# Attention with a fused feed-forward on one core: a column maximum taken by DVE block transposes and spread by a diagonal matmul

## The chip, the cores and the metric

One of the eight cores of a Trainium2 chip runs the whole program. The metric is the device time of one execution in microseconds. Five engines work side by side, each through its own list of instructions in order: PE (TensorE: matmuls and transposes), DVE (VectorE), ACT (ScalarE), POOL (GpSimd) and SP, which issues the DMAs. PSUM is the memory that PE writes; SBUF holds the rest.

## The reference

Attention over 8 batches and 8 heads, with the queries pooled in pairs, and behind it a feed-forward layer with a maximum of three products:

```python
q_pool = q.reshape(B, H, S // 2, 2, D).mean(axis=3)          # B 8, H 8, S 1152, D 64
scores = scale * np.matmul(q_pool, k.transpose(0, 1, 3, 2))  # 576 x 1152 for each head
scores = scores - np.max(scores, axis=-1, keepdims=True)
attn = np.exp(scores)
attn = attn / (np.sum(attn, axis=-1, keepdims=True) + 1e-09)
attn_out = np.matmul(attn, v)
x = attn_out.transpose(0, 2, 1, 3).reshape(B * S_pooled, H * D)   # 4608 tokens x 512
h = np.maximum(np.maximum(x @ w1, x @ w2), x @ w3)                # 512 -> 768
out = h @ w_out                                                   # 768 -> 512
```

All of it in float32.

## The kernel before, in words

**Tiling.** The attention is cut into 64 units, numbered d = 0 to 63: a batch (8), a pair of heads (4), and a half of 288 of the 576 pooled queries (2). In a unit the scores lie transposed: the 128 partitions are keys, the columns are 2 heads x 288 queries = 576. Nine blocks of 128 keys (`kk`) make up the 1152 keys. The feed-forward runs in chunks of 512 tokens, each once the batch that holds its tokens is done; the chunks are fitted between the units of the next batch, and the last of them follow behind the last unit.

**A unit.** For each `kk`, PE multiplies keys and queries into the PSUM tile `pqk`. Queries and keys are split into a high and a low part in float32r (lines 542 and 543: four matmuls of 288 columns for each `kk`). ACT copies `pqk` to the SBUF tile `s` (line 548), and DVE folds it into the running maximum `acc` (lines 554 and 557), one tile of 128 x 576 that exists once (`bufs=1`).

After the ninth block, `acc` holds a maximum over every 128th key, and what is wanted is the maximum over its partitions, for each of the 576 columns, and that in all partitions, because it has to be subtracted from `s`. This is done in two halves `h` of 345 and 231 columns, that is 3 and 2 blocks of 115:

- `rows` (line 593): PE transposes each block of `acc` into the PSUM tile `pmt`, so that a column becomes a partition;
- `reduce` (line 599, step `red`): DVE takes the maximum along the free axis into `m`, one number for each query;
- `bcast` (line 609, step `bc`): PE transposes `m`, repeated 128 times, into the PSUM tile `pmb`, so that each partition holds all the maxima of the half.

Both PSUM tiles of half 0 take the one buffer of `ps_a`, those of half 1 the one buffer of `ps_b`. Half 1 also waits until ACT has copied the attention output of the unit before out of `ps_b` (`xout[d - 1]`).

Then DVE subtracts (`sub`, line 624), ACT takes the exponential (`exp`, line 630), six pieces each. POOL adds the nine blocks of `s` into `ksum` (`key`, lines 643 and 645); PE multiplies `s` by the values into `pav` (`product` in `values`, line 673: 18 products, 36 matmuls), and sums `ksum` over the partitions with a matmul of ones (`total`, line 687). DVE takes the reciprocal (line 694), POOL scales (line 697), ACT and POOL split the result into `xh` and `xl` (lines 772 and 775) for the feed-forward. Up to unit 15 (`EARLY`) the sums are taken in another way, with small matmuls. `s` has six buffers of three blocks, enough for two units.

The feed-forward multiplies with split weights: `ph` (line 935) for the three inner products, `po` (line 990) for the outer one. With chunk 0, which runs beside units 8 and on, the weights are converted from 64-bit floats, mostly on DVE.

**Order.** The instructions are not issued in the order of the loops. Each piece of work is a `Step` with the engine that can do it, a cost in us, and the steps it has to follow. `arrange` is a list scheduler: it plays the steps through with these costs and picks, whenever an engine is free, the ready step with the lowest rank. The rank is the unit's number plus an offset for the kind of step (`RANK`) plus one for the single step (`NUDGE`). The order that comes out is fixed for each engine; on the chip an engine waits where an operand is late. The DMAs of the queries, keys, values and weights are issued by SP in that order too; POOL issues none.

Of the kernel before, what the change touches and what calls it, by code (L numbers as in the profile page):

```python
# [18 lines left out]
P = 128  # L19
# [3 lines left out]
QH = 288  # L23
CB = 115
DM = 512
# [11 lines left out]
    "qk": -364.0396,  # L37
    "cp": -126.5549,
    "mx": -318.2574,
    "rows": -969.9796,  # L40
    "red": -172.0313,
    "bc": -345.8464,
    "sub": 215.1752,
    "exp": 196.9402,
    "keys": -671.9276,
    "av": 14.8431,
    "xcopy": -516.1778,
    "psum": 398.4083,
    "eps": 343.2889,
    "inv": 357.0576,  # L50
    "xm": -706.0274,
    "load": 386.6538,
    "prep": 638.9001,
    "move": 1290.4425,
    "split": 283.1141,
    "ffn": -33.8173,
    "rate": 1.047,
    "mm": 49.0387,
    "fetch": 603.0832,
    "evac": -724.5554,  # L60
    "hhigh": 1228.3483,
    "hlow": -714.7034,
    "conv": 648.8915,
    "rate0": 4.5084,
    "first_qk": -97.1625,
    "first_cp": -630.79,
    "first_mx": 212.4188,
    "first_sub": 204.5779,
    "first_exp": 244.1512,
    "first_keys": -1118.9276,  # L70
    "first_av": 141.406,
    "first_xcopy": -152.0387,
    "first_psum": 65.359,
    "first_inv": 141.5566,
    "first_xm": 829.3378,
    "first_load": -197.5173,
    "first_prep": 180.1798,
    "first_move": -1436.3679,
    "first_split": 375.0794,
# [209 lines left out]
def pe(n):  # L289
    return ("pe", n * 1e-3)  # L290
# [784 lines left out]
```

## Time and profile before

| | |
|---|---|
| median of 3 runs | 1474.91 us (1472.44 to 1477.5) |
| profiled execution, its own time | 1472.96 us |
| span of the profiled execution, first to last instruction | 1471.1 us |
| mean granted clock of PE | 0.978 |
| PE busy | 1398.0 us (95%) |
| weight loads (PEld) | 1098.5 us (75%) |
| DVE busy | 1044.0 us (71%) |
| ACT busy | 902.5 us (61%) |
| POOL busy | 1079.1 us (73%) |

How to read the rows that follow. PE, PEld, DVE, ACT, POOL and SP are the engines; PEld is the loading of weights, which overlaps the matmuls. `L593` is line 593 of the kernel. A group row reads: line, engine, operation, output <- inputs, shape of the output <- shape of the first input, count | busy us, mean ns of one | us in which the engine was idle just before, and for whom it waited. A timeline row reads: start in us, length in us, engine, line, operation, tiles, count, and in brackets the idle time before. A wait row reads: who waited <- for whom: us in all, times, longest. The granted clock is the share of its full clock that PE was allowed. In a row by stretches the stretch and its length come first, then for PE, PEld, DVE, ACT and POOL the busy time with the number of instructions. Matmul ends are modelled and overlap, so a busy PE is not PE at its peak.

### The profile page before, as it was taken

Reading aid. Unit: us, or ns where it says so; the run is one execution under the profiler, and the core shown is the slowest. Engines: PE = TensorE matmul, PEld = TensorE weight load, DVE = VectorE, ACT = ScalarE, POOL = GpSimd, SP = SyncE. Lnnn points to the kernel's source line nnn. Section 1 sums busy time; section 2 is a strip of 40 time slices with the busy share of each in tenths; the row PEclk is TensorE's granted clock in tenths of the full one; section 3 lists DMA queues with packets and bytes.
Section 4 is the critical chain, followed back from the end, with each engine's and each line's share of the span. In section 5 each row is a group of like instructions: output and inputs, shape, how many; then the busy total and the mean of one; then the engine's idle time right before and its main releaser. Section 6 shows DMA issues by size and latency. Waiting matters only on the chain.

```text
span 1471.1 us, 24704 instructions
## 1 busy us (share of the span) xinstructions
PE 1398.0 (95%) x8704; PEld 1098.5 (75%) x8704; DVE 1044.0 (71%) x1441; ACT 902.5 (61%) x1464; POOL 1079.1 (73%) x835
## 2 busy tenths in 40 slices
PE   4888999898899999999999999999999999999999
PEld 4566677675677878777777777777777777878999
DVE  3897789898877767777688778777787768861110
ACT  3776776567666666567566766666766757651211
POOL 1897975889868878679888878888787978772210
PEclk9988999998899999999999999999999999999999
DMA  6675456576456656565567556664566556414441
GB/s 181 169 203 147 122 153 207 184 206 194 118 151 185 201 155 182 168 181 148 148 192 203 152 145 191 182 182 134 163 189 184 149 148 185 144 69 162 149 161 59
DMA packets 114762, 240.71 MB, mean 164 GB/s; under 512 B 15440, under 2 KB 75216, under 8 KB 114640
## 3 DMA queue, kind: packets, MB, share of 16 engines
q1 hardware_dynamic: 114064, 238.55, 55.8%
q8 instruction: 70, 1.15, 0.3%
q10 hardware_dynamic: 576, 0.59, 0.2%
q14 instruction: 52, 0.43, 0.1%
HBM read 144.70 MB, written 18.87 MB: 111 GB/s over the span
## 4 chain that ended last, share of the span: by engine, by line
PE 75%; DVE 10%; DMA 4%; ACT 4%; issue 4%; POOL 2%; SPq 1%; ACTq 0%; DVEq 0%; POOLq 0%
PE ph L935 28%; PE pav L673 14%; PE po L990 10%; PE pqk L542 9%; PE pqk L543 8%; DVE s L624 3%; DVE acc L557 3%; DMA kraw<-in_kT_dram 2%; PE pmt L593 2%; PE psum L687 2%; PE pmb L609 2%; POOL ksum L645 1%; ACT s L548 1%; DVE w L848 1%; DVE w L843 1%
## 5 line engine op out<-in xcount | busy, mean ns | idle before, releaser
L645 POOL TENSOR_TENSOR ksum<-ksum,s 128x576 f32<-128x576 f32 x448 | 638.2, 1425 | 26.1 <-ACT s L630 3.5
L935 PE MATMUL ph<-xh,w 128*128 128x512 f32 (+2 forms) x1440 | 464.3, 376 | 2.7 <-DVE w L868 1.3
L548 ACT COPY s<-pqk 128x576 f32<-128x576 f32 x576 | 362.4, 639 | 103.4 <-PE pqk L543 97.8
L624 DVE TENSOR_TENSOR s<-s,pmb 128x693 f32<-128x693 f32 (+1 forms) x384 | 395.1, 1049 | 39.5 <-PE pmb L609 38.3
L542 PE MATMUL pqk<-qq,kc 128*128 128x288 f32 x1152 | 357.9, 326 | 56.1 <-DVE acc L557 30.7
L557 DVE TENSOR_TENSOR acc<-acc,pqk 128x576 f32<-128x576 f32 x448 | 335.3, 749 | 82.8 <-ACT s L548 78.1
L630 ACT ACTIVATE s<-s 128x693 f32<-128x693 f32 (+1 forms) x384 | 352.5, 933 | 41.9 <-DVE s L624 38.6
L543 PE MATMUL pqk<-qq,kc 128*128 128x288 f32 x1152 | 332.3, 303 | 0.0
L542 PEld LDWEIGHTS pqk<-qq,kc 128*128 128x128 f32 x1152 | 225.6, 196 | 113.7 <-DVE acc L557 44.5
L673 PE MATMUL pav<-s,v 128*64 128x288 f32 x2304 | 306.8, 418 | 1.3 <-ACT s L630 1.0
L935 PEld LDWEIGHTS ph<-xh,w 128*128 128x128 f32 x1440 | 263.1, 188 | 41.4 <-ACT xr L682 1.8
L935 PE MATMUL ph<-xl,w 128*128 128x512 f32 (+2 forms) x720 | 268.3, 373 | 0.0
L673 PEld LDWEIGHTS pav<-s,v 128*64 128x64 f32 x2304 | 165.2, 140 | 119.3 <-issue 16.6
L543 PEld LDWEIGHTS pqk<-qq,kc 128*128 128x128 f32 x1152 | 227.5, 197 | 10.4
L643 POOL TENSOR_TENSOR ksum<-s 128x576 f32<-128x576 f32 x64 | 92.0, 1437 | 107.8 <-ACT s L630 104.8
L956 DVE TENSOR_TENSOR hm<-hm,ph 128x512 f32<-128x512 f32 (+2 forms) x120 | 75.8, 631 | 126.8 <-PE ph L935 124.8
L966 POOL TENSOR_TENSOR h_lo<-hm,h_hi 128x512 fp32r<-128x512 f32 (+2 forms) x60 | 70.6, 1176 | 126.1 <-ACT h_hi L963 123.6
L935 PEld LDWEIGHTS ph<-xl,w 128*128 128x128 f32 x720 | 135.8, 189 | 11.5
L438 POOL TENSOR_TENSOR kraw<-kraw 128x1152 fp32r<-128x1152 f32 x31 | 82.8, 2670 | 63.1 <-DMA qraw<-in_qT_dram 26.6
L599 DVE TENSOR_REDUCE m<-pmt 116x3 f32<-116x384 f32 (+1 forms) x128 | 61.3, 488 | 89.9 <-PE pmt L593 89.8
L682 ACT COPY xr<-pav 128x288 f32<-128x288 f32 x64 | 25.5, 399 | 147.0 <-PE pav L673 146.9
L694 DVE RECIPROCAL rs<-rs 128x288 f32<-128x288 f32 (+1 forms) x64 | 96.5, 1507 | 17.7 <-ACT rs L691 17.3
(57 smaller groups left out, 1293.6 us busy)
## 6 DMA issues: line engine op xcount, KB each, us to landing
w<-w_split SPq DMA_DIRECT2D x144, 512.0 KB, 3.6
kc<-kraw SPq DMA_DIRECT2D x384, 96.0 KB, 2.2
qq<-qraw SPq DMA_DIRECT2D x252, 144.0 KB, 3.3
v<-in_vr_dram SPq DMA_DIRECT2D x32, 576.0 KB, 3.8
kraw<-in_kT_dram SPq DMA_DIRECT2D x31, 576.0 KB, 6.0
qraw<-in_qT_dram SPq DMA_DIRECT2D x31, 576.0 KB, 4.0
w<-in_win_dram SPq DMA_DIRECT2D x18, 512.0 KB, 5.9
w_split<-w SPq DMA_DIRECT2D x18, 512.0 KB, 5.5
```

The lines of the kernel that those rows point to most:

```text
L542: nc.tensor.matmul(ps[:, h - hs[0], :QH], w, qq[:, 0, h], start=True, stop=False)
L543: nc.tensor.matmul(ps[:, h - hs[0], :QH], w, qq[:, 1, h], start=False, stop=True)
L548: nc.scalar.copy(o.s[kk // 3][:, kk % 3, slice(*hs)], o.ps[kk, hs][:, :, :QH])
L557: nc.vector.tensor_tensor(acc, acc, ps, op=ALU.max)
L624: nc.vector.tensor_tensor(s, s, o.pb[h][:, None, :w].broadcast_to([P, 3, w]), op=ALU.subtract)
L630: nc.scalar.activation(s, s, AF.Exp, scale=SCALE)
L643: vec[e].tensor_tensor(o.ksum, o.s[0][:, 0], x, op=ALU.add)
L645: vec[e].tensor_tensor(o.ksum, o.ksum, x, op=ALU.add)
L673: nc.tensor.matmul(o.pav[64 * h : 64 * h + 64, :QH], pr.v[:, kk, h], o.s[kk // 3][:, kk % 3, h], start=(kk == 0), stop=(kk == NK - 1),)
L694: nc.vector.reciprocal(o.rs, o.rs)
L935: nc.tensor.matmul(t.ps[:, : hi - lo], w[:, a, kk], xx[:, kk, lo:hi], start=(kk == 0 and i == 0), stop=(kk == 3 and i == 2),)
L990: nc.tensor.matmul(t.ps[:, : hi - lo], ww[:, kk, ms], hh[:, kk, lo:hi], start=(kk == 0 and i == 0), stop=(kk == 5 and i == 2),)
```

## The change

From unit 16 (`TURN`) on, `rows`, `reduce` and `bcast` are replaced:

- `fold`: one DVE reduction over `acc`, seen as 18 blocks of 32 columns, with `apply_transpose`. It transposes 32 x 32 blocks, so that the maximum is taken over each group of 32 partitions. The result, in `crest`, is 128 partitions x 18: partition 32 g + q, column t holds the maximum over partition group g for column 32 t + q.
- `turn`: one PE transpose of `crest`, 128 x 128, into `ps_a`.
- `summit`: one DVE reduction over the four groups, 18 x 32 maxima in PSUM.
- `m_high` on ACT and `m_low` on DVE split them into a high and a low float32r part, in partitions 0 to 17 and 32 to 49 of `parts2`.
- `spread_out`: one POOL multiplication of `pick` (a diagonal, both parts below each other) with `parts2` makes `diag`, 64 x (18 x 32), which is zero except where the row is the block's own.
- `bcast_wide`: two matmuls of a matrix of ones (`wide`, 128 x 128) with halves of `diag`, 288 columns each, put the sum of both parts into all 128 partitions. The halves are now 288 and 288 columns.

The next unit's first maximum into `acc` now waits for `fold` instead of both `rows`. `blank`, a DVE step at about unit 12, sets `pick` and zeroes the new tiles. Units 0 to 15 keep the old way. All numbers in `RANK` and `NUDGE` are others, so the order of every step can differ; the scheduler and its cost model are the same. The host code gives the program a smaller scratch for DMA descriptors.

```diff
+SQ = 32
+NB = 18
+TURN = 16
...
+    wide = cpool.tile([P, P], F32R, name="wide")
+    nc.vector.memset(wide.bitcast(F32), 1.0)
+    pick = cpool.tile([2 * SQ, NB], F32, name="pick")
+    crest = [cpool.tile([P, P], F32, name=f"crest{i}") for i in range(2)]
+    parts2 = [cpool.tile([2 * SQ, SQ], F32R, name=f"parts{i}") for i in range(2)]
+    diag = [cpool.tile([P, NB, SQ], F32R, name=f"diag{i}") for i in range(2)]
+
+    def blank():
+        for i in range(2):
+            rows = slice(SQ * i, SQ * i + SQ)
+            nc.vector.tensor_copy(pick[rows], ident[rows, SQ * i : SQ * i + NB])
+            nc.vector.memset(crest[i], 0.0)
+            nc.vector.memset(parts2[i].bitcast(F32), 0.0)
+            nc.vector.memset(diag[i].bitcast(F32), 0.0)
...
+    blanks = step("top", TURN - 4, [("dve", 3.2)], lambda e: blank(), [])
...
-                    after = [c] + ([copies[0]] + (old.rows if old else []) if kk == 1 else [tops[-1]])
+                    after = [c] + ([copies[0]] + (old.accread if old else []) if kk == 1 else [tops[-1]])
...
-        for h, (x0, x1) in enumerate([(0, 3 * CB), (3 * CB, 2 * QH)]):
+        late = d >= TURN
+        spans = [(0, QH), (QH, 2 * QH)] if late else [(0, 3 * CB), (3 * CB, 2 * QH)]
+        free_a = old.subs[0] if old else []
...
+        def fold(e):
+            nc.vector.tensor_reduce(
+                crest[d % 2][:, :NB],
+                o.acc.rearrange("p h q -> p (h q)").rearrange("p (t k) -> p t k", t=NB),
+                axis=AX.X, op=ALU.max, apply_transpose=True,
+            )
+
+        def turn(e):
+            o.pb[0] = ps_a.tile([P, 512], F32, tag="a", name=f"pmb{d}_0")
+            nc.tensor.transpose(o.pb[0][:, QH : QH + P], crest[d % 2], ident)
+
+        def summit(e):
+            o.top = o.pb[0][:NB, QH + P : QH + P + SQ]
+            nc.vector.tensor_reduce(
+                o.top, o.pb[0][:NB, QH : QH + P].rearrange("p (g k) -> p k g", g=4), axis=AX.X, op=ALU.max
+            )
+
+        def m_high(e):
+            nc.scalar.copy(parts2[d % 2][:NB], o.top)
+
+        def m_low(e):
+            nc.vector.tensor_tensor(parts2[d % 2][SQ : SQ + NB], o.top, parts2[d % 2][:NB], op=ALU.subtract)
+
+        def spread_out(e):
+            nc.gpsimd.tensor_tensor(
+                diag[d % 2][: 2 * SQ],
+                pick[:, :, None].broadcast_to([2 * SQ, NB, SQ]),
+                parts2[d % 2][:, None, :].broadcast_to([2 * SQ, NB, SQ]),
+                op=ALU.mult,
+            )
+
+        if late:
+            x = step("red", d, [("dve", 0.775)], fold, [tops[-1], blanks, getattr(old2, "turned", None)])
+            o.accread = [x]
+            x = o.turned = step("turn", d, [pe(150)], turn, [x] + free_a)
+            x = step("top", d, [("dve", 0.25)], summit, [x])
+            y = step("top", d, [("act", 0.2)], m_high, [x] + getattr(old2, "full", []))
+            x = step("top", d, [("dve", 0.17)], m_low, [x, y] + getattr(old2, "full", []))
+            full = step("diag", d, [("pool", 1.16)], spread_out, [x, y] + getattr(old2, "bcs", []))
...
+            def bcast_wide(e, h=h):
+                if h:
+                    o.pb[h] = ps_b.tile([P, 512], F32, tag="b", name=f"pmb{d}_{h}")
+                half = diag[d % 2][:, NB // 2 * h : NB // 2 * h + NB // 2]
+                nc.tensor.matmul(o.pb[h][:, :QH], wide, half.rearrange("p t k -> p (t k)"), start=True, stop=True)
...
+            if late:
+                b = step("bc", d + 0.1 * h, [pe(145)], bcast_wide, [full, gone] + (old.subs[1] if h else []), cols=QH)
```

More of the change, by code (lines that the diff above doesn't have):

```diff
@@ L36 @@
 RANK = {
[L37 to L79, printed above, removed]
+    "qk": -486.7374,
+    "cp": -103.3155,
+    "mx": -288.9473,
+    "rows": -790.567,
+    "turn": -659.5712,
+    "top": -182.8625,
+    "diag": -294.5856,
+    "red": -185.4375,
+    "bc": -601.717,
+    "sub": -61.1511,
+    "exp": 460.2444,
+    "keys": -280.409,
+    "av": -26.5486,
+    "xcopy": -292.3542,
+    "psum": 615.1834,
+    "eps": 886.2793,
+    "inv": 80.4537,
+    "xm": -555.9621,
+    "load": 502.0497,
+    "prep": 791.2287,
+    "move": 1196.0834,
+    "split": 125.478,
+    "ffn": 89.1205,
+    "rate": 5.3966,
+    "mm": 187.8282,
+    "fetch": 1021.9249,
+    "evac": -862.1647,
+    "hhigh": 563.7857,
+    "hlow": -491.662,
+    "conv": 581.7571,
+    "rate0": 6.3552,
+    "first_qk": 117.0643,
+    "first_cp": -304.3318,
+    "first_mx": -78.9748,
+    "first_sub": 607.3251,
+    "first_exp": -247.6462,
+    "first_keys": -231.2583,
+    "first_av": 681.3599,
+    "first_xcopy": -315.4183,
+    "first_psum": 75.5781,
+    "first_inv": 571.8784,
+    "first_xm": 774.8629,
+    "first_load": -542.1866,
+    "first_prep": -282.0663,
+    "first_move": -1397.9498,
+    "first_split": 676.8054,
 }
 NUDGE = {
[81 rows of a table removed]
[85 rows of a table added]
 }
@@ L585, in scores @@
         pools = (ps_a, ps_b)
-        for h, (x0, x1) in enumerate([(0, 3 * CB), (3 * CB, 2 * QH)]):
+        late = d >= TURN
+        spans = [(0, QH), (QH, 2 * QH)] if late else [(0, 3 * CB), (3 * CB, 2 * QH)]
+        free_a = old.subs[0] if old else []
+        bc = {}
+        def fold(e):
+            nc.vector.tensor_reduce(
+                crest[d % 2][:, :NB],
+                o.acc.rearrange("p h q -> p (h q)").rearrange("p (t k) -> p t k", t=NB),
+                axis=AX.X,
+                op=ALU.max,
+                apply_transpose=True,
+            )
[26 more added lines that the diff above has]
+            full = step("diag", d, [("pool", 1.16)], spread_out, [x, y] + getattr(old2, "bcs", []))
+            o.full = [full]
+            o.bcs = []
+        for h, (x0, x1) in enumerate(spans):
             nb, w = 3 - h, x1 - x0
@@ L613, in bcast @@
                     )
-            gone = xout[d - 1] if d > SPLIT and h else None
-            x = step("rows", d + 0.1 * h, [pe(133 * nb)], rows, [tops[-1], gone] + (old.subs[h] if old else []))
-            o.rows.append(x)
-            x = step("red", d, [("dve", 0.067 + nb * 0.133)], reduce, [x])
-            b = step("bc", d + 0.1 * h, [pe(89 + 99 * nb)], bcast, [x])
+            def bcast_wide(e, h=h):
+                if h:
+                    o.pb[h] = ps_b.tile([P, 512], F32, tag="b", name=f"pmb{d}_{h}")
+                half = diag[d % 2][:, NB // 2 * h : NB // 2 * h + NB // 2]
+                nc.tensor.matmul(
+                    o.pb[h][:, :QH], wide, half.rearrange("p t k -> p (t k)"), start=True, stop=True
+                )
+            gone = xout[d - 1] if d > SPLIT and h else None
+            if late:
+                b = step("bc", d + 0.1 * h, [pe(145)], bcast_wide, [full, gone] + (old.subs[1] if h else []), cols=QH)
+                o.bcs.append(b)
+            else:
+                x = step(
+                    "rows", d + 0.1 * h, [pe(133 * nb)], rows, [tops[-1], gone] + (old.subs[h] if old else [])
+                )
+                o.rows.append(x)
+                x = step("red", d, [("dve", 0.067 + nb * 0.133)], reduce, [x])
+                b = step("bc", d + 0.1 * h, [pe(89 + 99 * nb)], bcast, [x])
             for i in range(3):
@@ L635, in scores @@
                 o.exps[i, h] = step("exp", r, [("act", 0.109 + w / 400)], exp, [x])
+        if not late:
+            o.accread = o.rows
         o.sums = []
@@ L1059 @@
     from concourse.bass_utils import run_bass_kernel_spmd
-    nc = bacc.Bacc("TRN2", target_bir_lowering=False, num_devices=1)
+    nc = bacc.Bacc("TRN2", target_bir_lowering=False, num_devices=1, dynamic_dma_scratch_size=1024)
     arrays, args = {}, []
```

166 rows, old and new, of the table NUDGE are left out of this document.

## The prediction

> **What bounds the kernel now.** I read the page first, then the busy time by stretches of the span, then TensorE's own timeline, because the change takes TensorE work away and adds work to the other engines.
>
> ```profile
> span 1471.1 us, 24704 instructions
> PE 1398.0 (95%) x8704; PEld 1098.5 (75%) x8704; DVE 1044.0 (71%) x1441; ACT 902.5 (61%) x1464; POOL 1079.1 (73%) x835
> ```
>
> Busy time by stretch (columns: PE, PEld, DVE, ACT, POOL, granted clock, DMA share, GB/s):
>
> ```profile
> 0.00:300.00 300.00, 251.44 (x1636) 187.40 (x1636) 242.49 (x405) 198.50 (x316) 220.52 (x163) 0.94 0.59 168
> 200.00:300.00 100.00, 91.28 (x588) 70.13 (x586) 93.15 (x171) 65.06 (x111) 72.66 (x53) 0.98 0.61 187
> 300.00:400.00 100.00, 86.22 (x530) 63.98 (x530) 92.05 (x163) 70.99 (x123) 86.78 (x71) 0.86 0.64 185
> 400.00:1311.00 911.00, 903.55 (x5561) 700.81 (x5560) 681.12 (x831) 599.66 (x958) 730.64 (x560) 1.00 0.58 166
> ```
>
> From 400 us on TensorE is busy 903.55 of 911 us at full clock; DVE has 230 us free there, ACT 311, POOL 180. TensorE is the bound in that stretch, so what it sheds there should shorten the span. Before 400 us it isn't: between 200 and 400 us DVE is busy 92 to 93% and TensorE waits, with a clock that drops to 0.86. The transposes that the change removes, counted by stretch (PE columns first), say where the changed units lie:
>
> ```profile
> 0.00:300.00 300.00, 11.41 (x70) 8.11 (x70) 12.82 (x28) 0.94 0.59 168
> 300.00:400.00 100.00, 5.21 (x25) 3.16 (x25) 4.66 (x10) 0.86 0.64 185
> 400.00:1311.00 911.00, 40.38 (x225) 26.27 (x225) 43.58 (x90) 1.00 0.58 166
> ```
>
> Five `pmt` transposes belong to a unit: 14 units lie before 300 us, 5 between 300 and 400, 45 behind. Units 16, 17 and 18 are thus changed in the stretch that DVE holds, and 45 of the 48 changed units where TensorE is the bound.
>
> **The change part by part.** *Removed from TensorE.* A duration is not what an instruction occupies, since matmuls overlap; the starts tell. Two places, one of each kind:
>
> ```profile
> 845.73 0.39 PE L990 MATMUL po<-h_lo,wo_hi 128*128 128x512 f32 x1
> 845.96 0.39 PE L990 MATMUL po<-h_hi,wo_lo 128*128 128x512 f32 x1
> 846.19 0.49 PE L593 MATMUL pmt<-ident,acc 128*116 128x128 f32 x3
> 846.43 0.38 PE L542 MATMUL pqk<-qq,kc 128*128 128x288 f32 x1
> 846.65 0.29 PE L543 MATMUL pqk<-qq,kc 128*128 128x288 f32 x1
> 846.78 0.29 PE L542 MATMUL pqk<-qq,kc 128*128 128x288 f32 x1
> ...
> 872.12 0.29 PE L543 MATMUL pqk<-qq,kc 128*128 128x288 f32 x1
> 872.25 0.66 PE L609 MATMUL pmb<-ident,m 116*128 116x116 f32 x5
> 872.68 0.48 PE L935 MATMUL ph<-xh,w 128*128 128x512 f32 x1
> 873.00 0.40 PE L935 MATMUL ph<-xl,w 128*128 128x512 f32 x1
> ```
>
> A `po` matmul occupies 0.23 us (845.73 to 845.96) and a `pqk` 0.13 (846.65 to 846.78). From 845.96 to the second `pqk` are 0.69 us; less 0.23 and 0.13, three transposes cost 0.33, or 0.11 each. The first `pqk` behind them is included, as it starts early and takes longer. From 872.12 to the second `ph` are 0.88 us; less 0.13 and 0.23 (a `ph` has the 512 columns of a `po`), five `pmb` cost 0.52, or 0.104 each. A unit sheds 5 x 0.11 + 5 x 0.104 = 1.07 us.
>
> *Added to TensorE.* One transpose `turn` of 128 columns: from 0.11 (as now) to 0.12 (0.11 x 128/116); I take 0.12. Two matmuls of 288 float32r columns with 128x128 weights: that is the shape of `pqk`, 0.13 each. The upper end is that they run in two passes as `pav` does, 36 matmuls for 18 products:
>
> ```profile
> 705.95 4.59 PE L673 MATMUL pav<-s,v 128*64 128x288 f32 x36
> ```
>
> That is 0.255 a product. I take 0.13, since weights and moving operand are float32r as in `pqk`. Net per unit: 1.07 - 0.12 - 0.26 = 0.69 us; 45 units make 31.0 us; with the two-pass price it would be 0.44, or 20 us. For the three units between 300 and 400 us I count half of 2.1, 1 us.
>
> *DVE, ACT, POOL.* Rows of units 40 to 47, by shape, and single rows of the whole span:
>
> ```profile
> L593 PE MATMUL pmt<-ident,acc 128*116 128x128 f32 x42 | 7.7, 280 | 0.7 <-ACT xr L682 0.7
> L609 PE MATMUL pmb<-ident,m 116*128 116x116 f32 x40 | 6.6, 266 | 0.0
> L557 DVE TENSOR_TENSOR acc<-acc,pqk 128x576 f32<-128x576 f32 x56 | 41.9, 749 | 7.9 <-ACT s L548 7.2
> L599 DVE TENSOR_REDUCE m<-pmt 116x3 f32<-116x384 f32 x8 | 4.5, 557 | 14.2 <-PE pmt L593 14.2
> L599 DVE TENSOR_REDUCE m<-pmt 116x2 f32<-116x256 f32 x8 | 3.4, 423 | 1.9 <-PE pmt L593 1.9
> L772 ACT CAST xh<-xr 128x32 fp32r<-128x32 f32 x4 | 0.9, 218 | 0.0
> L645 POOL TENSOR_TENSOR ksum<-ksum,s 128x576 f32<-128x576 f32 x56 | 79.8, 1425 | 2.7
> ...
> L714 DVE TENSOR_SCALAR rs<-psum 96x6 f32<-96x6 f32 x16 | 2.4, 152 | 1.8 <-PE psum L704 1.7
> L338 DVE MEMSET ones<- 128x64 f32 x1 | 0.1, 112 | 0.8 <-PEq L1061 0.8
> L340 DVE MEMSET eps<- 128x1 f32 x1 | 0.1, 59 | 0.0
> ```
>
> DVE sheds two reductions, 0.557 + 0.423 = 0.98 us. It gains the fold over 576 elements: the two reductions grow by 0.134 per 128 elements, so 576 make 0.76; no row has the block-transposing form, and twice that, 1.5, is my upper end, for a pass of its own for the transpose. `top` reads 128 elements from PSUM: 0.29 by the same line. `m_low` is a small subtraction: 0.15 to 0.2. Together 1.25, so 0.27 more, 12 us in the 45 units, against 230 free: hidden by TensorE. With the upper end it is 45 us, still hidden. ACT gains `m_high`, 0.22 us, 10 us against 311. POOL gains `spread_out`, 576 elements from two inputs: the 1.43 us of `ksum`; the diff's planner puts 1.16, the lower end. That is 64 us, so POOL would be busy 795 of some 880 us, 90% instead of 80%. The cover is POOL's 180 free us; without it, each unit pays 1.43.
>
> The second half's `bc` keeps its waits for the copied `pav` of the unit before and for that unit's subtractions. The `sub` and `exp` pieces become 864 wide instead of 1035 and 693, the same elements: nothing.
>
> `blank` puts memsets and copies on DVE near unit 12, where DVE is the bound: from 0.112 and 0.059 a memset costs 0.06 + 0.84 ns an element, so 128, 576 and 32 wide with a small copy, twice, 1.8 us; I count 2 in full. `wide` is set at the start behind the first loads. The scratch size changes no instruction, and no DMA is added or moved past another.
>
> *The longer chain and the waits.* Now a unit's maximum goes DVE, PE, DVE, PE, DVE, in two halves that overlap. Then it goes DVE (0.76), PE (0.12), DVE (0.29), ACT (0.22), DVE (0.2), POOL (1.43), PE (0.13): 3.2 us without the handovers, and POOL works in order, so `spread_out` also waits for the `ksum` additions queued before it, up to 1.43 us for each. Behind a waiting `bc` on TensorE stand the next `pqk` or `ph`, and all six `sub` wait for it. What covers it is seen in unit 43:
>
> ```profile
> 886.16 0.75 DVE L557 TENSOR_TENSOR acc<-acc,pqk 128x576 f32<-128x576 f32 x1
> 887.31 0.54 PE L593 MATMUL pmt<-ident,acc 128*116 128x128 f32 x3
> 888.31 4.59 PE L673 MATMUL pav<-s,v 128*64 128x288 f32 x36
> 892.82 0.51 PE L609 MATMUL pmb<-ident,m 116*128 116x116 f32 x3
> 893.37 1.23 DVE L624 TENSOR_TENSOR s<-s,pmb 128x1035 f32<-128x1035 f32 x1 [3.07 <-PE pmb L609]
> ```
>
> From the end of the last maximum (886.91) to the first subtraction are 6.5 us, filled by a whole `pav`. The order leaves room for 3.2 us plus one or two queued additions. One stall goes: the next unit's first maximum waits today until both `pmt` groups have read `acc`; the fold reads it at once, on DVE itself. Its victims in units 40 to 47:
>
> ```profile
> PEld pqk L542 <- DVE acc L554: 1.8, 1, 1.8
> PE pqk L542 <- DVE acc L554: 1.4, 1, 1.4
> ```
>
> That is at most some 3 us in eight units, one event each, so I don't count it. For new waits I take 4 us: TensorE's idle 7.45 us between 400 and 1311 us half as much again. Ends: 0, and 31 (one 0.69 us wait in every unit).
>
> *The order.* Every rank and nudge changes, so the whole list is ordered anew, also before 400 us, where nothing else changes. TensorE is idle 62 us there (48.6 and 13.8). The dependencies and durations stay; I take 0 and as ends an eighth of it, 8 us either way.
>
> Sum against the profiled execution (span 1471.1, its own time 1472.96): -31.0 - 1 + 2 + 4 + 0 = -26, so 1447. The median of the three runs is 1474.91, 1.95 above, so 1449.
>
> **A rule against the row.** The Trainium skill, "TensorE: Matmul & The Clock Gate", Part 4, puts a PE transpose of 128x128 in a kernel's context at about 275 ns. The durations here, 280 and 266 ns, agree, the starts do not: 110 and 104 ns. Worked by its figure, ten transposes less one and two matmuls of 0.13 would be 2.2 us a unit, an estimate of 99 us in all.
>
> **The rivals.** *Durations count, not starts.* Then a unit sheds 5 x 0.280 + 5 x 0.266 = 2.73 and gains 0.28 + 2 x 0.29: 1.87 us, 84 us in 45 units, 1391. Against it: starts 0.11 apart in rows where TensorE never rests. Chance 0.01.
>
> *The new order is better too.* The freed `acc` wait and 8 us of the early idle come on top, and the 4 us aren't paid: about 1435. For it: 62 us of idle are there to be taken. Chance 0.14.
>
> *POOL eats half.* `spread_out` comes late in half of the units by the 0.69 us they save: 15 us back, 1464. For it: POOL at 90%. Chance 0.09.
>
> *No change that counts.* The same in every unit, 31 us back: about 1476. Also what comes out if the bound was not TensorE's work; 903.55 of 911 speaks against it. Chance 0.06.
>
> *Slower.* `spread_out` stands behind one `ksum` addition more than the order can hide, in every unit: 1.43 - 0.69 = 0.74 us lost, 33 us, 1507. It decides from 0.69 us a unit. For it: POOL's queue is in order and full of 1.43 us pieces, and its free time today is mostly waiting for work:
>
> ```profile
> POOL ksum L643 <- ACT s L630: 104.8, 38, 7.0
> DVE s L624 <- PE pmb L609: 38.3, 32, 3.1
> ```
>
> Against it: DVE waits for the spread maximum only 38.3 us in the span today, and TensorE, as in unit 43, has `pav` and `ph` to do meanwhile. Chance 0.08. Its price grows if the clock drops, as it does to 0.86 between 300 and 400 us where TensorE waits. The same page of the Trainium skill, Part 1, says that the clock halves after an idle window of about 3.4 us; the rows agree that it falls only where TensorE has gaps.
>
> **How the numbers follow.** The forecast's own case, 1440 to 1458, has 0.62; with the others: better order 0.14, durations 0.01, half eaten 0.09, no change 0.06, slower 0.08. I predict 1449. The range runs from 1430 (better order, with the earlier ends) to 1466 (half eaten) and leaves out about 0.18. Within 0.3%, 4.4 us, is about what a measurement of this kernel can't tell from no change. Faster by more: 0.62 + 0.14 + 0.01 + 0.09 = 0.86; same 0.06; slower 0.08.
>
> **What the profile after would show.** Right: 80 transposes left in each of the groups of `pmt` and `pmb`, 48 of the new kind, 96 new matmuls 0.13 us apart; eight steady units some 5 us shorter; TensorE still busy at least 98% of the steady stretch at clock 1.00; POOL near 90% with 48 new pieces of 1.2 to 1.45 us; a fold of 0.7 to 0.9 us. Wrong: new matmuls 0.25 apart; waits of TensorE for POOL's `diag`, or of DVE's `sub` for the spread maximum, well above 38 us; a fold above 1.5 us that holds up the maxima; or a different time to the start of unit 16, which would be the order's doing and not the maximum's.

## The result and the profile after

The changed kernel takes 1451.47 us (median of 4 runs, 1449.37 to 1456.11), against 1473.68 for the kernel before beside it (4 runs, 1471.57 to 1477.5). The ratio is 0.9851, with a 95% interval of 0.9818 to 0.9884: 22 us faster, where 24 to 26 were forecast (1449). The profiled execution is the slowest of the four, 1456.11 us, so the rows below show 17 us of the 22. In them TensorE is busy 27.0 us less (1371.0 against 1398.0) and idle 10.2 us more (83.3 against 73.1 of the span).

The head of its page, and the busy time by stretches (columns as before):

```profile
span 1454.3 us, 24119 instructions
PE 1371.0 (94%) x8368; PEld 1073.8 (74%) x8368; DVE 1058.9 (73%) x1498; ACT 907.0 (62%) x1512; POOL 1130.0 (78%) x883
...
0.00:300.00 300.00, 248.97 (x1598) 184.82 (x1600) 237.76 (x395) 196.43 (x308) 223.75 (x165) 0.92 0.56 162
300.00:400.00 100.00, 87.53 (x532) 64.20 (x529) 89.88 (x165) 66.77 (x120) 76.45 (x59) 0.89 0.66 197
400.00:500.00 100.00, 92.53 (x545) 69.61 (x545) 80.54 (x109) 67.87 (x111) 86.81 (x71) 0.95 0.56 159
500.00:1300.00 800.00, 791.03 (x4726) 615.36 (x4725) 613.30 (x777) 537.45 (x899) 694.23 (x545) 1.00 0.58 171
```

The same two late stretches of the kernel before:

```profile
400.00:500.00 100.00, 100.00 (x621) 77.80 (x620) 72.78 (x89) 63.28 (x96) 74.72 (x54) 1.00 0.57 163
500.00:1300.00 800.00, 792.55 (x4869) 615.14 (x4868) 600.81 (x734) 529.70 (x847) 645.00 (x498) 1.00 0.59 168
```

TensorE is still the bound from 500 us on: 791 of 800 us busy, as before, while POOL went from 645 to 694. What changed is what TensorE does in that time. The attention does not end sooner: the last `pav` matmul starts at 1328.8 us, before at 1324.8. But the feed-forward is further on. Matmuls of `ph` and then of `po` up to 1320 us, first of before, then of after:

```profile
0.00:1320.00 1320.00, 402.04 (x1512) 0.98 0.58 167
0.00:1320.00 1320.00, 124.67 (x474) 0.98 0.58 167
...
0.00:1320.00 1320.00, 412.82 (x1562) 0.97 0.58 169
0.00:1320.00 1320.00, 131.12 (x504) 0.97 0.58 169
```

80 more of them are done, which at a spacing of 0.23 us is 18 us. The time that the maximum no longer takes went to matmuls of the feed-forward, and the tail of feed-forward behind the last unit is shorter by that. The sign "eight steady units some 5 us shorter" is therefore not there: from the first maximum of unit 24 to that of unit 63 it is 794.5 us before and 793.7 after.

Another sign was the time to unit 16, the first changed one. Its first maximum, in the kernel before and in the changed one:

```profile
326.94 0.74 DVE L554 TENSOR_TENSOR acc<-s,pqk 128x576 f32<-128x576 f32 x1
327.39 0.74 DVE L579 TENSOR_TENSOR acc<-s,pqk 128x576 f32<-128x576 f32 x1
```

The time is the same, and by then 192 `ph` matmuls are done before and 168 after. So the new order has gained nothing where the maximum is still the old one.

The new steps as groups:

```profile
L617 DVE TRANSPOSE_TENSOR_REDUCE crest<-acc 128x18 f32<-128x576 f32 x48 | 36.7, 764 | 1.0
L627 PE MATMUL pmb<-ident,crest 128*128 128x128 f32 x48 | 15.2, 316 | 0.2 <-DVE crest L617 0.2
L631 DVE TENSOR_REDUCE pmb<-pmb 18x32 f32<-18x128 f32 x48 | 13.7, 285 | 48.4 <-PE pmb L627 48.4
L636 ACT CAST parts<-pmb 18x32 fp32r<-18x32 f32 x48 | 8.3, 173 | 6.3 <-DVE pmb L631 6.2
L639 DVE TENSOR_TENSOR parts<-pmb,parts 18x32 fp32r<-18x32 f32 x48 | 8.6, 180 | 15.1 <-ACT parts L636 14.6
L642 POOL TENSOR_TENSOR diag<-pick,parts 64x576 fp32r<-64x576 f32 x48 | 55.4, 1154 | 10.3 <-DVE parts L639 5.6 <-PE pqk L568 4.2 <-DMA qq<-qraw 0.6
L693 PE MATMUL pmb<-diag,wide 128*128 128x288 f32 x96 | 25.6, 325 | 8.5 <-POOL diag L642 4.4 <-ACT xr L772 4.1
```

And one unit's new work on TensorE, from its timeline:

```profile
906.09 0.30 PE L568 MATMUL pqk<-qq,kc 128*128 128x288 f32 x1
906.23 0.27 PE L627 MATMUL pmb<-ident,crest 128*128 128x128 f32 x1
906.26 0.48 PE L1025 MATMUL ph<-xh,w 128*128 128x512 f32 x1
906.58 0.40 PE L1025 MATMUL ph<-xl,w 128*128 128x512 f32 x1
...
910.58 0.29 PE L568 MATMUL pqk<-qq,kc 128*128 128x288 f32 x1
910.71 0.43 PE L693 MATMUL pmb<-diag,wide 128*128 128x288 f32 x2
910.97 0.40 PE L1025 MATMUL ph<-xh,w 128*128 128x512 f32 x1
911.21 0.39 PE L1025 MATMUL ph<-xl,w 128*128 128x512 f32 x1
```

Read as before: from 906.09 to the second `ph` are 0.49 us, less 0.13 and 0.23 leaves 0.13 for the transpose. From 910.58 to the second `ph` are 0.63, less the same leaves 0.27 for the two spreading matmuls. A unit's new maximum occupies 0.40 us of TensorE, the old one 1.07.

The place matters for a single one. Where the transpose stands between a `pav` and a `pqk` (22 of 48), the second `pqk` starts 0.64 us after the `pav` matmul, and 0.57 without a transpose between them: 0.07 us. Between a `psum` and a `pav` it is 0.60 instead of 0.24 to the second `pav`: 0.36 us, in 6 units. Taken like this over all places from 430 us on for which the trace has the like spacing without it, the mean of a unit is 0.42 us in the changed kernel and 1.08 in the kernel before: 0.66 saved.

### The profile page after: what moved, and what is told of

Same layout as the page of the kernel before. It is cut to its first block, busy times and chain, and to the rows that moved or that the text cites. A ratio compares the mean times of both kernels' runs of the same rounds, so it can differ in the third digit from the quotient of the medians.

```text
span 1454.3 us, 24119 instructions
## 1 busy us (share of the span) xinstructions
PE 1371.0 (94%) x8368; PEld 1073.8 (74%) x8368; DVE 1058.9 (73%) x1498; ACT 907.0 (62%) x1512; POOL 1130.0 (78%) x883
## 3 DMA queue, kind: packets, MB, share of 16 engines
q1 hardware_dynamic: 114064, 238.55, 55.4%
## 4 chain that ended last, share of the span: by engine, by line
PE 68%; DVE 10%; DMA 6%; POOL 6%; issue 4%; ACT 3%; SPq 2%; ACTq 0%; POOLq 0%; DVEq 0%
PE ph L1025 26%; PE pav L763 14%; PE po L1080 8%; PE pqk L567 8%; PE pqk L568 7%; DVE acc L582 3%; DVE s L712 3%; POOL ksum L735 2%; DMA qq<-qraw 2%; PE psum L777 2%; DMA w<-in_win_dram 1%; ACT s L573 1%; DMA kc<-kraw 1%; PE pmb L693 1%; ACT s L718 1%
## 5 line engine op out<-in xcount | busy, mean ns | idle before, releaser
L735 POOL TENSOR_TENSOR ksum<-ksum,s 128x576 f32<-128x576 f32 x448 | 637.9, 1424 | 26.6 <-ACT s L718 6.9
L712 DVE TENSOR_TENSOR s<-s,pmb 128x864 f32<-128x864 f32 (+2 forms) x384 | 394.2, 1047 | 33.9 <-PE pmb L693 31.0
L567 PE MATMUL pqk<-qq,kc 128*128 128x288 f32 x1152 | 350.2, 320 | 57.0 <-DVE acc L582 32.4
L718 ACT ACTIVATE s<-s 128x864 f32<-128x864 f32 (+2 forms) x384 | 351.0, 931 | 50.1 <-DVE s L712 47.8
L568 PE MATMUL pqk<-qq,kc 128*128 128x288 f32 x1152 | 332.9, 304 | 0.0
L763 PE MATMUL pav<-s,v 128*64 128x288 f32 x2304 | 311.6, 422 | 2.0 <-ACT s L718 1.7
L763 PEld LDWEIGHTS pav<-s,v 128*64 128x64 f32 x2304 | 168.3, 142 | 124.0 <-issue 16.6
L1025 PEld LDWEIGHTS ph<-xl,w 128*128 128x128 f32 x720 | 136.1, 189 | 10.6
L1080 PE MATMUL po<-h_hi,wo_hi 128*128 128x512 f32 (+2 forms) x240 | 89.1, 371 | 0.1
```

Source lines behind the costliest of these rows:

```text
L567: nc.tensor.matmul(ps[:, h - hs[0], :QH], w, qq[:, 0, h], start=True, stop=False)
L568: nc.tensor.matmul(ps[:, h - hs[0], :QH], w, qq[:, 1, h], start=False, stop=True)
L712: nc.vector.tensor_tensor(s, s, o.pb[h][:, None, :w].broadcast_to([P, 3, w]), op=ALU.subtract)
L718: nc.scalar.activation(s, s, AF.Exp, scale=SCALE)
L735: vec[e].tensor_tensor(o.ksum, o.ksum, x, op=ALU.add)
L763: nc.tensor.matmul(o.pav[64 * h : 64 * h + 64, :QH], pr.v[:, kk, h], o.s[kk // 3][:, kk % 3, h], start=(kk == 0), stop=(kk == NK - 1),)
```

## The experiments

Theory A: the gain is the TensorE time that the maximum no longer occupies, counted by starts, because TensorE is the bound. Rivals: it is the new order; transposes cost their durations; POOL has become a second bound that takes part of the gain. Differences below come from the ratios to the kernel before, which ran beside each of them, at 1473.7 us; the intervals of both ratios are combined.

**1. Five more transposes in each late unit.**

```diff
-            nc.tensor.transpose(o.pb[0][:, QH : QH + P], crest[d % 2], ident)
+            for _ in range(6):
+                nc.tensor.transpose(o.pb[0][:, QH : QH + P], crest[d % 2], ident)
```

> The changed kernel with its one transpose per late unit issued six times, order untouched: 240 more PE transposes. Theory A (TensorE is the bound and a transpose costs what its start spacing shows, 0.11 to 0.125 us): 26 to 30 us more than the changed kernel, about 1479. Rival B (a transpose costs its duration, 0.316 us in the trace): 76 us more, about 1527. Rival C (the gain came from the new order, TensorE has room): under 5 us more, about 1453.

1471.72 us, ratio 0.9995 (0.9979 to 1.0011): 21 us more than the changed kernel, give or take 5. The durations' 76 us are out, and so is a free TensorE. The 26 to 30 that were expected are a little high. By starts, the second `pqk` behind a `pav` comes 0.54 us later with six transposes than with one (1.18 and 0.64), and the second `ph` between `ph` matmuls too (1.12 and 0.58), so each added one costs 0.108, 26 us in all. That is at the upper end of the 21 with its interval. Five transposes put back eat the whole gain.

**2. The block-transposing reduction twice.**

```diff
-            nc.vector.tensor_reduce(
+            for _ in range(2):
+                nc.vector.tensor_reduce(
```

> The changed kernel with the block-transposing reduction issued twice, order untouched: 48 x 0.764 = 37 us more on DVE, and the chain to the first subtraction 0.76 us longer. Theory A (DVE is hidden behind TensorE): at most 6 us more, and that in the first late units, where DVE is the bound. Rival (DVE or the chain's length decides): 25 to 37 us more.

1464.69 us, ratio 0.9944 (0.9923 to 0.9965): 14 us more, give or take 6: neither expectation held. DVE isn't the bound, but 0.76 us in front of `turn` isn't free: TensorE, which waited 0.2 us for `crest` in all, now waits here 5.2 us between 500 and 1300 us:

```profile
PE pmb L628 <- DVE crest L618: 5.2, 18, 0.6
```

The profiled executions differ by 10.6 us, and 2.8 of these lie before unit 16, where both kernels run the same instructions: its first maximum starts at 330.2 us here and at 327.4 there. In the traces of runs 1 to 6, all alike up to that point, it lies between 322.6 and 330.2 us, so a single trace can't settle a difference of a few us. What the rest of the 14 us is stays open.

**3 and 4. The POOL multiplication twice, and three times.**

```diff
-            nc.gpsimd.tensor_tensor(
+            for _ in range(2):          # 3 in the second kernel
+                nc.gpsimd.tensor_tensor(
```

> The changed kernel with the POOL multiplication issued twice, order untouched: 48 x 1.154 = 55 us more on POOL, whose busy share of the steady stretch goes from 87 to 93%. Theory A (POOL is still covered): at most 10 us more. Rival (POOL has become a second bound, which took part of the gain): 30 to 55 us more.

> The changed kernel with the POOL multiplication issued three times: 111 us more on POOL, which would fill the steady stretch to 99%. Theory A: here POOL takes over, 25 to 65 us more, and less than proportional to the step before would be a surprise. Rival (POOL never matters, since TensorE has other work): under 10 us more.

1491.13 us, ratio 1.0128 (1.0111 to 1.0145), 41 us more (give or take 6) for 55 on POOL; and 1560.69 us, ratio 1.0592 (1.0565 to 1.0618), 109 more for 111, above both expectations. So theory A's cover is wrong here. TensorE's waits for the multiplication between 500 and 1300 us, in the changed kernel, with two and with three:

```profile
PE pmb L693 <- POOL diag L642: 1.1, 4, 0.5
...
PE pmb L694 <- POOL diag L643: 22.1, 30, 2.1
...
PE pmb L694 <- POOL diag L643: 56.8, 29, 3.3
```

And the same stretch, again in this order (the first of them is shown above):

```profile
500.00:1300.00 800.00, 771.48 (x4570) 596.31 (x4568) 596.31 (x751) 522.88 (x873) 719.71 (x568) 1.00 0.56 172
...
500.00:1300.00 800.00, 737.52 (x4239) 571.95 (x4238) 554.90 (x697) 486.73 (x808) 709.60 (x563) 0.96 0.53 159
```

POOL is busy 720 and 710 of 800 us. It isn't full even where it costs 109 us, so it is not POOL's sum that decides.

**5. The second multiplication where nobody waits for it.**

```diff
                     vec[e].tensor_tensor(o.ksum, o.ksum, x, op=ALU.add)
+                if kk == NK - 1 and late:
+                    spread_out(e)
```

> The changed kernel with the POOL multiplication issued a second time at the end of the unit, behind the unit's last addition, where no matmul waits for it; order untouched. The same 48 x 1.154 = 55 us more on POOL as in the run that doubled it in place, which cost some 40 us. Theory A (what costs is the place in front of the spreading matmuls, which the order times to the multiplication's end; POOL as a whole is covered): at most 15 us more than the changed kernel, up to about 1466. Rival B (POOL's total work is a second bound): 30 to 45 us more, about 1480 to 1496.

1467.8 us, ratio 0.9957 (0.9937 to 0.9977): 16 us more, give or take 6, at theory A's edge and far from the 41. POOL does the same work (1182.3 us busy, and 1184.4 with the doubling in place). So some 25 us of the 41 are the place in front of the spreading matmuls. The other 16 are in good part the same wait, likely because POOL's queue runs later, which is not shown. TensorE waits 12.4 us for `diag` in the stretch, where the changed kernel had 1.1:

```profile
PE pmb L693 <- POOL diag L642: 12.4, 13, 1.9
```

**6. Relief for POOL: the scaling on DVE.**

```diff
-            vec[e].tensor_tensor(xs, xs, o.rs, op=ALU.mult)
+            nc.vector.tensor_tensor(xs, xs, o.rs, op=ALU.mult)
```

> The changed kernel with the scaling of the attention output (0.80 us a unit) issued on DVE instead of POOL, order untouched: 38 us less on POOL, about 22 us more on DVE. Theory A (POOL's total is covered): within 5 us of the changed kernel, about 1446 to 1456. Rival B (POOL's total is a second bound at the price of the doubled multiplication, 40 us for 55): about 25 us less, 1426.

1458.4 us, ratio 0.9898 (0.9868 to 0.9928): 7 us more, give or take 7, not 25 less. But DVE paid more than the 22 us that were expected. The scaling there, and, from the changed kernel, DVE's like piece of units 0 to 15, whose second input lies in PSUM:

```profile
L787 DVE TENSOR_TENSOR xr<-xr,rs 128x288 f32<-128x288 f32 x48 | 52.7, 1099 | 1.0
...
L818 DVE TENSOR_TENSOR xr<-xr,psum 128x288 f32<-128x288 f32 x16 | 7.2, 448 | 1.6 <-PE psum L809 1.6
```

1099 ns against 448: 31 us more on DVE than priced. What DVE met is in the timeline, at two of the 48 scalings, with all that POOL did beside them:

```profile
439.93 1.42 POOL L735 TENSOR_TENSOR ksum<-ksum,s 128x576 f32<-128x576 f32 x1
440.24 1.43 DVE L787 TENSOR_TENSOR xr<-xr,rs 128x288 f32<-128x288 f32 x1
...
483.39 0.45 DVE L787 TENSOR_TENSOR xr<-xr,rs 128x288 f32<-128x288 f32 x1
```

The first ends 0.32 us behind POOL's addition. The second has no POOL instruction beside it and takes 0.45 us, like the one at 1316.89 (0.44). Of all the scalings, 42 end 0.29 to 0.34 us behind the end of a POOL instruction. The scaling waits for POOL, then, and POOL's busy time falls by 29 us instead of 38 (1130.0 to 1100.8). So this run refutes rival B's 25 us only as far as that doesn't hide it; what speaks against POOL's sum as a second bound is run 5, and POOL's free time in runs 3 and 4.

**7 and 8. The order without the maximum, the maximum without the order.**

```diff
-TURN = 16
+TURN = 64                       # kernel 7: new RANK and NUDGE, old maximum throughout, no blank
```

```diff
-RANK = {...new...}; NUDGE = {...new...}
+RANK = {...old, and new for turn, top, diag...}; NUDGE = {...likewise...}     # kernel 8, in short
```

> The changed kernel with the old maximum in all 64 units, but the new ranks and nudges: the order alone. Theory A (the gain is TensorE's shed work, and an order fits only the durations it was made for): no faster than before, 1473 to 1515. Rival (the new order is what gains): about 1451.

> The new maximum from unit 16 on with the ranks and nudges of the kernel before; only the three new kinds of step have the new kernel's values: the maximum alone. Theory A1 (shed work gains under any sensible order): 1445 to 1462. Theory A2 (the chain through POOL needs an order made for it): 1465 to 1500, no faster than before or slower, with TensorE waiting for POOL's multiplication and for DVE.

Kernel 7: 1501.26 us, ratio 1.0181 (1.0157 to 1.0206), 27 us slower than before. Kernel 8: 1485.37 us, ratio 1.0077 (1.0054 to 1.01), 11 us slower than before, though TensorE sheds the same work. Theory A2's time held, and one of its two waits. TensorE waits for DVE, as the rows show: between 500 and 1300 us in the kernel before, in the changed kernel and in kernel 8, and then kernel 8's stretch. For POOL's multiplication only weight loads wait in kernel 8, 1.2 us in the whole span.

```profile
PE pqk L542 <- DVE acc L557: 0.2, 1, 0.2
...
PE pqk L567 <- DVE acc L582: 5.0, 5, 1.7
...
PE pqk L704 <- DVE acc L719: 18.8, 24, 1.5
...
500.00:1300.00 800.00, 774.91 (x4509) 593.16 (x4510) 591.05 (x747) 520.47 (x866) 675.14 (x530) 0.97 0.56 169
```

TensorE waits for DVE to finish the running maximum before it may overwrite `pqk`. It is busy 775 of 800 us instead of 793, at a clock of 0.97. The gaps are only part of the loss: against the changed kernel, whose instructions on TensorE are as many, it is idle 10.9 us more over the span (94.2 against 83.3) and also busy 15.7 us longer (1386.7 against 1371.0), at a mean clock of 0.963 instead of 0.971. Neither part gains by itself. Each has been given an order that was made for the other maximum, though, so these two runs don't say what either is worth in an order of its own.

**9 and 10. Both maxima with an order searched alike.** Random changes to ranks and nudges were kept where they shortened the scheduler's own plan, two rounds of it for the old maximum and three for the new. Kernel 9 is the kernel before with such an order, kernel 10 the changed one, with the zeroing moved to the start (run 11 does that alone).

```diff
-RANK = {...}; NUDGE = {...}
+RANK = {...searched...}; NUDGE = {...searched...}
```

> The kernel before with its ranks and nudges searched anew by random moves that shorten the scheduler's own plan, two rounds of such a search; the maximum stays the old one. Theory A (most of the gain belongs to the shed TensorE work, and only a part to a better order): 1460 to 1470, so 3 to 13 us faster than before and at least 9 us slower than the changed kernel. Rival B (the old maximum, given the same care, does as well): 1447 to 1455.

> The changed kernel with its ranks and nudges searched in the same way, three rounds, and the zeroing of the new tiles at the start of the kernel, while DVE waits for the first loads. Theory A (the changed kernel lost some 10 us before 500 us to gaps and half clock, which an order can win back; the saved TensorE work stays): 1433 to 1445. Rival (the order is as good as the chip allows, a plan's gain doesn't carry over): 1446 to 1456.

On the same chip: the old maximum 1459.82 us, ratio 0.9896 (0.9875 to 0.9918); the new one 1440.08, ratio 0.9754 (0.9729 to 0.9779). Kernel 9 is 15 us faster than before and only 7, give or take 6, slower than the changed kernel, where theory A said at least 9. Two thirds of the 22 us are thus to be had with the old maximum, by a better order alone.

The difference between 9 and 10, 0.0142 give or take 0.0033, is 21 us (16 to 26). That is the best value here of the new maximum by itself; the third round for the new one, if anything, adds to it. Kernel 10 also has the smaller scratch and 9 has not, and no run sets that apart; in the kernel before and the changed one the main DMA queue moved the same 114064 packets, 238.55 MB. The traces of 9 and 10 fit the 21 us. Counted as in the result's section, a unit's maximum occupies 1.02 us in 9 and 0.44 in 10, which for 48 units is an estimate of 28 us. Against that, TensorE is idle 7.2 us more in 10 (70.6 against 63.4 of the span). The first 400 us, then 400 to 500, of 9 and of 10:

```profile
0.00:400.00 400.00, 343.03 (x2186) 258.04 (x2187) 327.70 (x562) 266.51 (x433) 304.74 (x231) 0.91 0.61 173
400.00:500.00 100.00, 100.00 (x606) 77.07 (x607) 74.43 (x91) 63.23 (x96) 73.46 (x53) 1.00 0.63 180
...
0.00:400.00 400.00, 339.92 (x2157) 253.03 (x2159) 337.14 (x580) 273.17 (x446) 311.91 (x236) 0.90 0.61 176
400.00:500.00 100.00, 99.11 (x579) 75.38 (x576) 77.07 (x101) 64.13 (x103) 80.74 (x60) 0.98 0.52 151
```

Kernel 10 is the fastest of all, 36 us below the kernel before. It has back what the changed kernel lost between 400 and 500 us, 99.11 busy instead of 92.53.

**11. The zeroing at the start.**

```diff
-    blanks = step("top", TURN - 4, [("dve", 3.2)], lambda e: blank(), [])
+    blank()
+    blanks = step("top", TURN - 4, [("dve", 3.2)], lambda e: None, [])
```

> The changed kernel with the zeroing of the new tiles moved from about unit 12 to the start, order otherwise untouched. Theory A (the 2 us counted in full for it, since DVE is the bound there): 1 to 3 us less, about 1449. Rival (it fell into a gap): within 1 us.

1452.39 us, ratio 0.9849 (0.9822 to 0.9875): no difference, and the trace of the changed kernel says why. There it stands at the start already:

```profile
1.34 0.16 DVE L361 COPY pick<-ident 32x18 f32<-32x18 f32 x1 [0.26 <-POOL ident masks.py:199]
...
2.81 0.54 DVE L364 MEMSET diag<- 128x576 f32 x1
4.01 0.46 DVE L448 TENSOR_TENSOR qraw<-qraw 128x288 f32<-128x288 f32 x1 [0.66 <-DMA qraw<-in_qT_dram]
```

The step follows nothing, so the scheduler takes it as soon as DVE is free, whatever its rank; DVE then still waits 0.66 us for the first load. The run is a repetition of the changed kernel, and the expectation rested on a wrong reading of the code.

**12. The transpose over 18 columns.**

```diff
-nc.tensor.transpose(o.pb[0][:, QH : QH + P], crest[d % 2], ident)
+nc.tensor.transpose(o.pb[0][:NB, QH : QH + P], crest[d % 2][:, :NB], ident)
```

> The changed kernel with its order searched anew, as in the run before, and the one transpose taken over the 18 columns of crest that are used instead of all 128: weights of 128 x 18, the 128 moving columns as before. Theory A (a transpose costs a weight load that scales with the weights' columns): the spacing of the new transpose falls from 0.11 to 0.03 us, 48 times, so 4 us less, about 1436. Theory B (it costs its moving columns and a fixed part): the spacing stays at 0.10 to 0.12 us and the time within 2 us of 1440.

1442.84 us, ratio 0.9783 (0.9758 to 0.9808), no gain over 10, as theory B expected. Between two `ph` the transpose occupies 0.113 us, in kernel 10 0.110, so the width of the weights is not what it pays for there. Right behind a `pav` it does save 0.05 us (0.587 against 0.638 to the second `pqk`), in 14 units, and as much in 7 more behind `psum` or `pav`: about 1 us in all, which the run can't show.

## Why the prediction was right, and where it wasn't

**Removed and added, right.** The new transpose took 0.12 to 0.13 us (taken 0.12) and the two matmuls 0.27 (taken 0.26) in the places that were read, and in the mean of the late units the saving is 0.66 us (taken 0.69). The starts, not the durations, give the price in place (run 1). The Trainium skill's 275 ns for a transpose ("TensorE: Matmul & The Clock Gate", Part 4) is thus no price of TensorE time here; as a duration it is near (316 ns).

**DVE, ACT, POOL, nearly right.** Fold 0.764 (0.76), `top` 0.285 (0.29), `m_low` 0.180 (0.15 to 0.2), `m_high` 0.173 (0.22). The multiplication took 1.154 us: the lower end, not the 1.43 that was chosen. POOL's share in the late stretch is 694 of 800, 87%, not 90.

**`blank`, wrong.** The 2 us were charged at unit 12, where DVE is the bound; the work ran in the first 4 us, behind nothing, and cost nothing.

**New waits, too small, and in another place.** 4 us were taken for the stretch from 400 us on, and 9 came. From 500 us on TensorE is idle 9.0 us where it was 7.5, so nearly nothing. Between 400 and 500 us it is idle 7.5 us where it was 0, with a clock of 0.95. The sign for it, waits of DVE for the spread maximum well above 38 us, isn't there:

```profile
DVE s L712 <- PE pmb L693: 31.0, 20, 3.7
```

The mechanism is as described: unit 43 has 6.2 us from its last maximum to its first subtraction, and TensorE has other work meanwhile. What the prediction did not see is how exactly the order is cut to the chain: 1.15 us more in it cost 41 us (run 3). The slower rival had the right mechanism and the right point, a fraction of a microsecond a unit; it did not happen, most likely because the order's cost for this piece, 1.16, is what the chip takes.

**The stall that goes** is seen. The kernel before waits for the first maximum of a unit (line 554) between 500 and 1300 us:

```profile
PEld pqk L542 <- DVE acc L554: 8.7, 6, 2.3
PE pqk L542 <- DVE acc L554: 6.5, 4, 1.9
```

The changed kernel has no such row in that stretch. But TensorE waits there 5.0 us for the later maxima (line 582), where it was 0.2 (the rows stand with run 8). It was counted at nothing, and in sum that is about right.

**The sum.** With what the runs gave it reads -30 (45 x 0.66), -1 for the three early units, which no run separates, 0 for `blank` and +9 for waits: -22, and 22 were measured. That the two misses, 2 us too much for `blank` and 5 too little for waits, nearly cancel is luck.

**The order, wrong in size.** The prediction took 0, with ends of 8 us either way. Runs 7 to 10 give its worth: the old order costs the new maximum 33 us (run 8 against the changed kernel, give or take 6), and a better order gains the old maximum 15. The forecast came out because the changed kernel brings an order that fits it; nothing in the prediction's sum told such an order from another, so in this term it was luck. The same maximum under the old ranks would have been 11 us slower than before, outside the range. What stays open is why TensorE is idle 7 us more in 10 than in 9: POOL's longer chain takes some of the freedom in placing work, but no run separates that from a search that stopped short.

## What to carry to other kernels

Price a TensorE instruction by what its presence adds between the starts of its neighbours, the first neighbour behind it included; ten transposes that last 0.28 us each were worth 0.11. Where a fixed order has been cut to measured durations, a shed instruction is worth its time only with an order made anew, and the fair comparison gives both versions the same search. Test a new link of a chain by doubling it in place and again off the chain: a share of busy time (87% here) says little about how much longer that link may get.

## What the runs showed of the hardware

The DVE reduction that transposes 32 x 32 blocks takes 764 ns for 128 x 576 float32, hardly more than a plain maximum of two operands of that size (748 ns): the transpose costs next to nothing. The POOL multiplication of 64 partitions x 576 with both inputs broadcast takes 1154 ns, where 128 x 576 from two full inputs takes 1424; these runs do not tell which of the two differences it is. A PE transpose of float32 between two `ph` costs TensorE 0.11 us whether its weights have 128 columns or 18. Between a `pav` and a `pqk` it costs 0.07, and between a `psum` and a `pav` 0.36.

A DVE multiplication with both inputs in SBUF took 1099 ns in the mean beside a busy POOL, 445 and 444 ns in the two cases where POOL was at rest, and 448 ns with one input in PSUM (run 6). The Trainium skill, "SBUF — State Buffer", section "Who interferes with whom", says that a DVE instruction with two SBUF inputs contends with a GpSimd instruction that reads SBUF, because its second input comes through the shared read interface, and that this contention is an exclusive lock. The trace agrees: beside a POOL addition of 1.42 us the multiplication ended 0.32 us behind the addition's end, whatever was left of it. In two places where the multiplication got ahead it took 0.44 us, and the addition beside it 1.79.
